# Attention, routed experts and a bilinear layer on one core: the last tokens' ranks, two weight loads, the w3 conversions and a padding moved

## The chip, the core and the metric

The kernel runs on one core of a Trainium2 chip. Its engines are TensorE (PE in the profile; PEld is its loading of weights), VectorE (DVE), ScalarE (ACT), GpSimd (POOL) and SyncE (SP), which here issues nearly all DMAs from one queue, in order. The metric is the device time of one execution in microseconds; less is better.

## The reference

Three layers follow each other, on 4 sequences of 576 tokens (N = 2304) with 512 features:

```python
# attention: 8 heads of 64, causal window of 128, linear bias per head, softmax
attn_out = _attn_ref(q, k, v)
x = attn_out.transpose(0, 2, 1, 3).reshape(B * S, H * D)

# experts: each token goes to one of 8
logits = x @ w_gate + modality_bias[modality_id]
e_idx = np.argmax(logits, axis=1)
gate_w = softmax(logits)[np.arange(N), e_idx]
for e in range(E):
    mask = e_idx == e
    h = np.maximum(x[mask] @ w1[e], 0.0)          # 512 -> 1024
    out[mask] = gate_w[mask, None] * (h @ w2[e])  # 1024 -> 512

# bilinear layer
a = x @ w1; b = x @ w2                            # 512 -> 1024
out = ((a * b) @ w3) @ w_out                      # 1024 -> 1024 -> 512
```

The weights of the bilinear layer come as float64 and are converted on the chip.

## The kernel before

All matrix products whose precision matters are done as three products of high and low parts: `split(hi, lo, src)` lets ACT write the high part (L264) and DVE the difference (L266), and `mm3` gives PE the three products (L281 to L283). A scheduler that simulates the engines orders the instructions of each engine from the order in the code and from `tc.issue_after(i)`, within which nothing is issued before the instruction i.

The stages of the program:

1. **Attention** (to about 222 us). For each unit (sequence, chunk of 128 tokens, four heads): scores, softmax, transposes, products with v. When a chunk is complete, `gate_logits(i, ...)` multiplies its output by the identity and the gate weights in one product (xlg); DVE multiplies by the reciprocal sums r and writes the token rows x and the gate's parts lh (L492); x goes to DRAM (xz, L502). Tiles 8 and 17 hold the 64-token tails of two sequences; there r is `one_r`, all ones, as the sums have been applied already. `route(g, ...)` takes a group of tiles: experts (hot_b, L531), counts before each tile (hcum, L536), ranks within the expert (rk, two products on PE, L540 and L543), positions (pos_i, L556), and scatters each token's number to its position in the list inv (POOL, L558). Group 4, the last, holds tiles 16 and 17.
2. **w3 times w_out** is prepared beside the attention, in pieces. `load_w3` brings piece i of w3 (float64, raw_w3_i; the profile writes raw_w) from DRAM by SP; `cvt_w3` converts it with five DVE instructions (w L694 and L698, p L701, x L704 and L707); `w3_transposes` has PE transpose it (w3tp_i, L739) and splits it (w3h_i, w3l_i); `w_step` adds its product to pw_j, which takes pieces 2j and 2j+1, and ACT copies pw out (wraw, L759). The list W_STEPS gives how many of these steps stand behind each attention unit; the rest follows behind the attention.
3. **The gap** (222 to 257 us). `block_table` computes from the counts which expert each block of 480 tokens takes (eb_i; eb0_i for the first), where its rows begin in the list (row_i, row0_i) and its columns (cols_i). SP reads these values from memory into registers (TENSOR_LOAD) before loads that depend on them: `load_w(g)` loads piece g of the expert weights (fw_g, 512 KB, L955), `gather_x(b)` loads block b's part of the list (ids_b, L975) and POOL gathers the token rows (xb, L981). `first_loads` issues the first list and then three pieces. `split_w` makes fwh and fwl of a piece, `block_transposes` transposes the gathered rows (btp, L1004) and splits them to xbh and xbl.
4. **Five blocks of experts** (257 to 450 us): ph and py are their products; the hidden part is kept in Whl. Beside them m's weights are converted.
5. **The bilinear layer** (to the end): products pS, pP, pA, pV, pG (L1296) with the weight pieces wth and wtl, and the output part po. Its weight pieces share their buffers with the expert pieces fwh and fwl (`f_p`).

SBUF is laid out by pools in stacks. `PAD` bytes per partition are reserved ahead of the pools of stages 3 to 5 on the left stack, so PAD moves all of their buffers.

Of the kernel before, what the change touches and what calls it, by code (L numbers as in the profile page):

```python
# [9 lines left out]
F32R = mybir.dt.float32r  # L10
# [4 lines left out]
ALU = mybir.AluOpType  # L15
# [3 lines left out]
P = 128  # L19
# [4 lines left out]
RU_LAST = 100  # L24
PAD = 32
NB_STATIC = 5
# [4 lines left out]
TP_AFTER = 20  # L31
LEAD = [4, 3, 1]
TS = 384
HB = 8
# [12 lines left out]
def kernel(  # L47
# [428 lines left out]
    def gate_logits(i, g, pos):  # L476
# [6 lines left out]
        for u in range(2):  # L483
            tp = pst("A", [P, 2, GW], f"xlg_{i}_{u}")
            for t in range(2):
                nc.tensor.matmul(
                    tp[:, t, :], lhsT=oT[:, 2 * u + t, :], rhs=wgx[:, 2 * u + t, :],
                    start=True, stop=True,
                )
            rr = r[:, 4 * u : 4 * u + 4].rearrange("p (t j o) -> p t j o", t=2, o=1)  # L490
            for dst, lo, n in ((lh, P, E), (x, 0, D)):
                nc.vector.tensor_tensor(  # L492
                    out=dst[:, 4 * u : 4 * u + 4, :].rearrange("p (t j) d -> p t j d", t=2),
                    in0=tp[:, :, lo : lo + 2 * n].rearrange("p t (j d) -> p t j d", j=2),
                    in1=rr.to_broadcast([P, 2, 2, n]), op=ALU.mult,
                )
# [7 lines left out]
    def route(g, i0, m):  # L504
# [30 lines left out]
        for j in range(i0, i0 + m):  # L535
# [6 lines left out]
        )  # L542
        nc.tensor.matmul(  # L543
            rk[:, :m, :], lhsT=ones_b, rhs=hcum[:, sl, :], start=False, stop=True
# [10 lines left out]
        )  # L555
        nc.vector.tensor_tensor(out=pos1_i[:, sl], in0=mn, in1=rank[:, sl], op=ALU.add)  # L556
        for j in range(i0, i0 + m):
# [175 lines left out]
    def w3_transposes(i):  # L733
        x = st_w.pop(("x", i))
        h = w_p.tile([P, 4, P], F32R, tag="w3h", name=f"w3h_{i}", bufs=3)
        l = w_p.tile([P, 4, P], F32R, tag="w3l", name=f"w3l_{i}", bufs=3)
        tp = pst("A", [P, 4, P], f"w3tp_{i}")
        for j in range(4):
            nc.tensor.transpose(tp[:, j, :], x[:, j * P : (j + 1) * P], ident)  # L739
        split(h, l, tp)  # L740
        st_w["last"] = (last["a"], last["v"])
        st_w["T", i] = (h, l)
# [127 lines left out]
    for i in range(nu + 2):  # L870
# [29 lines left out]
        for f in w_jobs.pop(i, []):  # L900
            f()
    todo += [lambda: None] * 4
    for i, f in enumerate(todo):
        f()
        for f in w_jobs.pop(nu + 2 + i, []):
            f()
    assert not w_jobs
    if j_in < n_j:
# [197 lines left out]

    def first_loads(b0, b1):

        gather_x(b0)
        with tc.issue_after(last["ids"].ins):  # L1110
            for g in range(b0 * NS, min(b0 * NS + LA, b1 * NS)):
                load_w(g)

    def run_blocks(b0, b1, extra, after=()):
# [8 lines left out]
        for b in range(b0, b1):  # L1123
            for s in range(NS):
                g = NS * b + s
                if g + LA < g1:
                    load_w(g + LA)
                if s == 0 and b + 1 < b1:
                    gather_x(b + 1)
                if s == 2:  # L1130
                    copy_ids(b)
# [19 lines left out]
    x_p = xstk.enter_context(tc.tile_pool(name="xp", bufs=2))  # L1151
    first_loads(0, NB_STATIC)
    for n in range(k_in, n_w):
        j, first = w_piece(n)
        if first:
            w3_transposes(j)
            if j + 2 < n_j:
                load_w3(j + 2)
            if j + 1 < n_j:
                cvt_w3(j + 1)  # L1160
        w_step(n)
# [104 lines left out]
    def split_wt(g, f, k):  # L1266
        h, l = (
            f_p.tile([P, 7, P], F32R, tag=f"w{x}", name=f"wt{x}_{g}_{f}_{k}", bufs=4) for x in "hl"
        )
        split(h, l, wt.pop(("raw", g, f, k)))  # L1270
        wt.setdefault((g, f), []).append((h, l))
# [287 lines left out]
```

## Time and profile before

| | |
|---|---|
| median of 3 runs | 762.26 us (760.52, 762.26, 768.61) |
| the profiled execution | 757.12 us |
| its span, first to last instruction | 755.4 us |
| mean granted clock of TensorE | 0.996 |
| PE busy | 734.9 us, 97% of the span |
| DVE busy | 526.2 us, 70% |
| ACT busy | 347.3 us, 46% |
| POOL busy | 74.9 us, 10% |
| DMA | 116.29 MB, 154 GB/s on average |

An engine's busy time is that of its instructions without the waits between them. The busy time of a pipelined instruction overlaps that of the next, so a distance from start to start can be shorter than the time of one. The granted clock is given as a share of 2.4 GHz.

### The profile page before, as it was taken

How to read it: one execution, taken by the hardware profiler on the slowest of the kernel's cores; microseconds unless marked ns; L12 is line 12 of the kernel's file. 1: busy time of each engine (PE TensorE's matmuls, PEld its weight loads, DVE VectorE, ACT ScalarE, POOL GpSimd, SP SyncE). 2: the span in 40 equal slices, each digit the busy share in tenths (PEclk: the TensorE clock that was granted, in tenths of full speed). 3: DMA queues.
4: the chain of work that ended last, by engine and by line, in shares of the span. 5: the costliest groups of instructions: out<-in, count | busy, mean ns of one | idle time of the engine just before them, and what ended most of it. 6: DMA issues, size and time to landing. Idle time of an engine off the chain costs nothing. (4 is left out here: it accounts for less than half of the span.)

```text
span 755.4 us, 12359 instructions
## 1 busy us (share of the span) xinstructions
PE 734.9 (97%) x4335; PEld 631.5 (84%) x4335; DVE 526.2 (70%) x1351; ACT 347.3 (46%) x778; POOL 74.9 (10%) x105
## 2 busy tenths in 40 slices
PE   7899999999999999999999999999999999999996
PEld 5777777787877788888888899999789997899984
DVE  3688888767689469697994347888657775568721
ACT  4787775866842533333343438231632315323221
POOL 5000200201013202030020000000120001100011
PEclk9999999999999999999999999999999999999999
DMA  7999467264136947979698344643226432233011
GB/s 132 325 312 252 109 179 178 67 161 129 44 84 149 253 144 222 293 196 352 180 297 268 132 133 116 209 123 98 77 71 192 123 96 77 67 118 116 1 43 42
DMA packets 126416, 116.29 MB, mean 154 GB/s; under 512 B 69631, under 2 KB 100735, under 8 KB 126344
## 3 DMA queue, kind: packets, MB, share of 16 engines
q1 hardware_dynamic: 122664, 105.91, 48.7%
q0 software_dynamic: 3680, 9.49, 4.0%
q8 instruction: 36, 0.59, 0.4%
q14 instruction: 36, 0.29, 0.1%
HBM read 87.69 MB, written 27.51 MB: 153 GB/s over the span
## 5 line engine op out<-in xcount | busy, mean ns | idle before, releaser
L264 ACT ACTIVATE wth<-wt 128x896 fp32r<-128x896 f32 x48 | 43.0, 946 | 89.6 <-PE pP L1296 89.6
L266 DVE TENSOR_TENSOR fwl<-fw,fwh 128x1024 fp32r<-128x1024 f32 x40 | 48.8, 1225 | 46.3 <-ACT fwh L264 45.8
L397 ACT ACTIVATE p<-p,mn 128x256 f32<-128x256 f32 (+2 forms) x144 | 68.1, 475 | 21.3 <-DVE mn L392 21.0
L264 ACT ACTIVATE fwh<-fw 128x1024 fp32r<-128x1024 f32 x40 | 42.1, 1062 | 76.6 <-PE ph L282 58.9
L281 PE MATMUL ph<-xbh,fwh 128*128 128x480 f32 (+1 forms) x160 | 60.1, 376 | 0.7 <-ACT xbh L264 0.7
L282 PE MATMUL py<-Whl,fwh 128*128 128x480 f32 (+1 forms) x160 | 59.9, 375 | 0.0
L282 PE MATMUL ph<-xbl,fwh 128*128 128x480 f32 (+1 forms) x160 | 59.7, 373 | 0.0
L283 PE MATMUL ph<-xbh,fwl 128*128 128x480 f32 (+1 forms) x160 | 59.6, 373 | 0.0
L283 PE MATMUL py<-Whl,fwl 128*128 128x480 f32 (+1 forms) x160 | 57.8, 373 | 0.0
L281 PE MATMUL po<-Whl,abh 128*128 128x512 f32 x144 | 57.1, 397 | 0.6 <-ACT abh L264 0.6
L283 PE MATMUL po<-Whl,abl 128*128 128x512 f32 x144 | 57.1, 398 | 0.0
L281 PE MATMUL py<-Whl,fwh 128*128 128x480 f32 (+1 forms) x160 | 56.9, 373 | 0.0
L282 PE MATMUL po<-Whl,abh 128*128 128x512 f32 x144 | 56.8, 394 | 0.0
L266 DVE TENSOR_TENSOR abl<-ab,abh 128x512 fp32r<-128x512 f32 x36 | 24.7, 690 | 40.7 <-ACT abh L264 40.6
L266 DVE TENSOR_TENSOR wtl<-wt,wth 128x896 fp32r<-128x896 f32 x48 | 51.8, 1083 | 1.6 <-ACT wth L264 1.4
L392 DVE CUSTOM_DVE_ANT_0 p<-S,bias 128x256 f32<-128x256 f32 (+1 forms) x128 | 43.8, 385 | 12.6 <-PE S L366 12.2
L1305 DVE TENSOR_TENSOR c<-pA,u 128x384 f32<-128x384 f32 x48 | 26.7, 557 | 33.9 <-PE pA L1296 31.7
L264 ACT ACTIVATE abh<-ab 128x512 fp32r<-128x512 f32 x36 | 22.5, 630 | 57.6 <-PE po L282 40.2
L454 PE MATMUL av<-pT,vr 128*64 128x128 f32 (+2 forms) x576 | 47.9, 275 | 0.0
L1401 POOL DMA_INDIRECT out_dram<-o,sid x18 | 21.6, 1200 | 262.9 <-ACT o L1400 262.9
L454 PEld LDWEIGHTS av<-pT,vr 128*64 128x64 f32 (+1 forms) x576 | 32.5, 136 | 11.5 <-issue 5.0
L418 PE MATMUL PT<-ident,p 128*128 128x128 f32 x224 | 41.0, 290 | 0.3
(256 smaller groups left out, 1944.6 us busy)
## 6 DMA issues: line engine op xcount, KB each, us to landing
wt<-wT SPq DMA_DIRECT2D x48, 448.0 KB, 3.3
fw<-in_moe_w_dram SPq DMA_DIRECT2D x40, 512.0 KB, 4.2
raw_w<-in_moe_w_dram SPq DMA_DIRECT2D x16, 512.0 KB, 5.1
raw_m<-in_moe_w_dram SPq DMA_DIRECT2D x32, 256.0 KB, 5.4
wT<-ms SPq DMA_DIRECT2D x16, 448.0 KB, 5.4
yT<-zf SPq DMA_DIRECT2D x20, 256.0 KB, 5.8
x<-yT SPq DMA_DIRECT2D x12, 384.0 KB, 5.5
vr<-in_v_dram SPq DMA_DIRECT2D x16, 256.0 KB, 4.6
```

Of the source, the lines that this page charges most:

```text
L264: last["a"] = nc.scalar.activation(out=hi, in_=src, func=AF.Copy, scale=scale)
L266: last["v"] = nc.vector.tensor_tensor(out=lo, in0=src, in1=f32(hi), op=ALU.subtract)
L281: nc.tensor.matmul(dst, lhsT=lh, rhs=rh, start=start, stop=False)
L282: nc.tensor.matmul(dst, lhsT=lh, rhs=rl, start=False, stop=False)
L283: return nc.tensor.matmul(dst, lhsT=ll, rhs=rh, start=False, stop=stop)
L392: nc.vector.tensor_tensor_reduce(out=p[:, j, t, :nk], in0=s[j][:, t, :nk], in1=bi, scale=1.0, scalar=BIG, op0=ALU.add, op1=ALU.min, accum_ ...
L397: nc.scalar.activation(out=p[:, j, t, :nk], in_=p[:, j, t, :nk], func=AF.Exp, scale=-1.0, bias=m1, accum_out=sm[:, col : col + 1],)
L418: nc.tensor.transpose(pt[:, t, kb, :], p[:, j, t, kb * P : (kb + 1) * P], ident)
L454: nc.tensor.matmul(av[j * D : (j + 1) * D, hp, cs], lhsT=raw["v", b, cc][:n_k, 2 * hp + j, :], rhs=rhs, start=(i_k == 0), stop=(i_k == len ...
L1305: last["d"] = nc.vector.tensor_tensor(out=out, in0=in0, in1=in1, op=op)
L1401: sc = nc.gpsimd.indirect_dma_start(out=out, out_offset=bass.IndirectOffsetOnAxis(ap=sid[g][:, j, 0:1], axis=0), in_=o, in_offset=None, bo ...
```

## The change

- In `gate_logits` x of the two tiles with r = one_r is copied by ACT, in two parts each, and no longer multiplied on DVE.
- `route` of the last group is taken out of the row of attention jobs and called ahead of the jobs of number `W_RANK` = 43, within an `issue_after` on the last transpose of the piece before; all later w3 jobs stand behind the last rank product (`last["rk"]`).
- The conversions of w3's pieces from j_in + 1 on are issued behind the last positions (`last["pos"]`).
- `first_loads` issues two weight pieces (SA = 2) and then the first list, in place of the list and three pieces (LA = 3). In `run_blocks` the next block's list is issued ahead of further weight pieces.
- PAD goes from 32 to 416 bytes. The tiles of the bilinear layer's weight pieces take the full slot of 1024 elements, and the pieces stand in it from element `WT_PAD` = 32 on. By the addresses, the offsets of fw, fwh and fwl within 512 bytes go from 416 to 288, those of xb, xbh and xbl from 480 to 352, those of the ab buffers from 96 to 480; wth and wtl stay at 416.

```diff
@@ -22,7 +22,8 @@
 NU, RU = 4, 120
 BLK = NU * RU
 RU_LAST = 100
-PAD = 32
+PAD = 416
+WT_PAD = 32
 NB_STATIC = 5
 NB_MAX = 12
 PE_LO = 9
@@ -30,6 +31,7 @@
 WO_AT = [9, 9, 12, 12, 12, 12, 14, 15]
 TP_AFTER = 20
 LEAD = [4, 3, 1]
+W_RANK = 43
 TS = 384
 HB = 8
 JS, BT = (2, 1)
@@ -488,7 +490,11 @@
                     start=True, stop=True,
                 )
             rr = r[:, 4 * u : 4 * u + 4].rearrange("p (t j o) -> p t j o", t=2, o=1)
-            for dst, lo, n in ((lh, P, E), (x, 0, D)):
+            if r is one_r:
+                nc.scalar.copy(
+                    x[:, 4 * u : 4 * u + 4, :].rearrange("p (t j) d -> p t (j d)", t=2), tp[:, :, :P]
+                )
+            for dst, lo, n in ((lh, P, E), (x, 0, D))[: 1 if r is one_r else 2]:
                 nc.vector.tensor_tensor(
                     out=dst[:, 4 * u : 4 * u + 4, :].rearrange("p (t j) d -> p t j d", t=2),
                     in0=tp[:, :, lo : lo + 2 * n].rearrange("p t (j d) -> p t j d", j=2),
@@ -540,7 +546,7 @@
         nc.tensor.matmul(
             rk[:, :m, :], lhsT=tri_b, rhs=hot_b[:, sl, :], start=True, stop=False
         )
-        nc.tensor.matmul(
+        last["rk"] = nc.tensor.matmul(
             rk[:, :m, :], lhsT=ones_b, rhs=hcum[:, sl, :], start=False, stop=True
         )
         nc.vector.tensor_reduce(out=sm, in_=ex, axis=AX.X, op=ALU.add)
@@ -553,7 +559,9 @@
         nc.vector.tensor_scalar(
             out=mn, in0=mn, scalar1=float(E), scalar2=float(CAP), op0=ALU.add, op1=ALU.mult
         )
-        nc.vector.tensor_tensor(out=pos1_i[:, sl], in0=mn, in1=rank[:, sl], op=ALU.add)
+        last["pos"] = nc.vector.tensor_tensor(
+            out=pos1_i[:, sl], in0=mn, in1=rank[:, sl], op=ALU.add
+        )
         for j in range(i0, i0 + m):
             sc = nc.gpsimd.indirect_dma_start(
                 out=inv2, out_offset=bass.IndirectOffsetOnAxis(ap=pos1_i[:, j : j + 1], axis=0),
@@ -736,7 +744,7 @@
         l = w_p.tile([P, 4, P], F32R, tag="w3l", name=f"w3l_{i}", bufs=3)
         tp = pst("A", [P, 4, P], f"w3tp_{i}")
         for j in range(4):
-            nc.tensor.transpose(tp[:, j, :], x[:, j * P : (j + 1) * P], ident)
+            st_w["t"] = nc.tensor.transpose(tp[:, j, :], x[:, j * P : (j + 1) * P], ident)
         split(h, l, tp)
         st_w["last"] = (last["a"], last["v"])
         st_w["T", i] = (h, l)
@@ -899,12 +907,19 @@
             todo.pop(0)()
         for f in w_jobs.pop(i, []):
             f()
-    todo += [lambda: None] * 4
-    for i, f in enumerate(todo):
+
+    *todo, route_last = todo
+    for f in todo:
         f()
-        for f in w_jobs.pop(nu + 2 + i, []):
+    for i in sorted(w_jobs):
+        if i == W_RANK:
+            with tc.issue_after(st_w["t"].ins):
+                route_last()
+            behind_rank = ExitStack()
+            behind_rank.enter_context(tc.issue_after(last["rk"].ins))
+        for f in w_jobs.pop(i):
             f()
-    assert not w_jobs
+    behind_rank.close()
     if j_in < n_j:
         load_w3(j_in)
         cvt_w3(j_in)
@@ -1104,12 +1119,11 @@
 
     LA, SA = 3, 2
 
-    def first_loads(b0, b1):
-
-        gather_x(b0)
-        with tc.issue_after(last["ids"].ins):
-            for g in range(b0 * NS, min(b0 * NS + LA, b1 * NS)):
-                load_w(g)
+    def first_loads():
+
+        for g in range(SA):
+            load_w(g)
+        gather_x(0)
 
     def run_blocks(b0, b1, extra, after=()):
         g0, g1 = b0 * NS, b1 * NS
@@ -1123,10 +1137,11 @@
         for b in range(b0, b1):
             for s in range(NS):
                 g = NS * b + s
-                if g + LA < g1:
-                    load_w(g + LA)
                 if s == 0 and b + 1 < b1:
                     gather_x(b + 1)
+                for n in range(SA if g == g0 else LA, LA + 1):
+                    if g + n < g1:
+                        load_w(g + n)
                 if s == 2:
                     copy_ids(b)
                 if g + SA < g1:
@@ -1149,7 +1164,7 @@
 
     xstk = ExitStack()
     x_p = xstk.enter_context(tc.tile_pool(name="xp", bufs=2))
-    first_loads(0, NB_STATIC)
+    first_loads()
     for n in range(k_in, n_w):
         j, first = w_piece(n)
         if first:
@@ -1157,7 +1172,8 @@
             if j + 2 < n_j:
                 load_w3(j + 2)
             if j + 1 < n_j:
-                cvt_w3(j + 1)
+                with tc.issue_after(last["pos"].ins) if j > j_in else nullcontext():
+                    cvt_w3(j + 1)
         w_step(n)
     w3_last = st_w["last"]
     wstk.close()
@@ -1265,7 +1281,10 @@
 
     def split_wt(g, f, k):
         h, l = (
-            f_p.tile([P, 7, P], F32R, tag=f"w{x}", name=f"wt{x}_{g}_{f}_{k}", bufs=4) for x in "hl"
+            f_p.tile([P, 2 * DM], F32R, tag=f"w{x}", name=f"wt{x}_{g}_{f}_{k}", bufs=4)[
+                :, WT_PAD : WT_PAD + 7 * P
+            ].rearrange("p (s c) -> p s c", s=7)
+            for x in "hl"
         )
         split(h, l, wt.pop(("raw", g, f, k)))
         wt.setdefault((g, f), []).append((h, l))
```

The first place is **PE** between the two halves of product pw_4. Here rk_4 are the ranks, w3tp_9 the transposes of piece 9, w3h_9 and w3l_9 its parts, tri_b and ones_b constants. Before:

```order
L283 MATMUL pw_4_3300<-woh_110,w3l_8_3258 128x512
L540 LDWEIGHTS tri_b_74
L540 MATMUL rk_4_3323<-hot_b_86,tri_b_74 128x16
L739 MATMUL w3tp_9_3344<-ident_70,x_w3_9_3268 128x128 x4
L543 LDWEIGHTS ones_b_73
L543 MATMUL rk_4_3323<-hcum_85,ones_b_73 128x16
L281 MATMUL pw_4_3300<-woh_110,w3h_9_3342 128x512
L282 MATMUL pw_4_3300<-wol_111,w3h_9_3342 128x512
```

After:

```order
L285 MATMUL pw_4_3300<-woh_110,w3l_8_3258 128x512
L747 MATMUL w3tp_9_3315<-ident_70,x_w3_9_3268 128x128 x4
L546 LDWEIGHTS tri_b_74
L546 MATMUL rk_4_3338<-hot_b_86,tri_b_74 128x16
L549 LDWEIGHTS ones_b_73
L549 MATMUL rk_4_3338<-hcum_85,ones_b_73 128x16
L283 MATMUL pw_4_3300<-woh_110,w3h_9_3313 128x512
L284 MATMUL pw_4_3300<-wol_111,w3h_9_3313 128x512
```

The transposes stood between the two rank products; they now stand ahead of both.

The second place is **DVE** from the rank products to the first values of the block table. Of w3's pieces, w_w3, p_w3 and x_w3 are the steps of a conversion; pr and rank lead to the positions pos1_i, f0 and cm belong to the block table. Before:

```order
L704 SCALAR_TENSOR_TENSOR x_w3_12_3530<-raw_w3_12_3494,p_w3_12_3529 128x512
L550 TENSOR_TENSOR pr_4_3310<-rk_4_3323,onehot_84 128x16
L266 TENSOR_TENSOR w3l_9_3343<-w3tp_9_3344,w3h_9_3342 128x512
L707 TENSOR_TENSOR x_w3_12_3530<-x_w3_12_3530,w_w3_12_3528 128x512
L701 TENSOR_SCALAR p_w3_13_3561<-w_w3_13_3560 128x512
L551 TENSOR_REDUCE rank_83<-pr_4_3310 128x2
L577 SCALAR_TENSOR_TENSOR fe_3378<-cnt_3376,iota_em_81 128x8
L586 COPY cnt_s_3384<-cnt_3376 128x8
L694 TENSOR_SCALAR w_w3_14_3592<-raw_w3_14_3558 128x512
L556 TENSOR_TENSOR pos1_i_82<-mnx_4_3313,rank_83 128x2
L580 TENSOR_REDUCE f0_3379<-fe_3378 128x1
L589 TENSOR_TENSOR cm_3389<-cnt_s_3384,thr_113 128x40
```

After:

```order
L556 TENSOR_TENSOR pr_4_3325<-rk_4_3338,onehot_84 128x16
L268 TENSOR_TENSOR w3l_9_3314<-w3tp_9_3315,w3h_9_3313 128x512
L557 TENSOR_REDUCE rank_83<-pr_4_3325 128x2
L585 SCALAR_TENSOR_TENSOR fe_3378<-cnt_3376,iota_em_81 128x8
L594 COPY cnt_s_3384<-cnt_3376 128x8
L562 TENSOR_TENSOR pos1_i_82<-mnx_4_3328,rank_83 128x2
L702 TENSOR_SCALAR w_w3_12_3526<-raw_w3_12_3492 128x512
L588 TENSOR_REDUCE f0_3379<-fe_3378 128x1
L597 TENSOR_TENSOR cm_3389<-cnt_s_3384,thr_113 128x40
L702 TENSOR_SCALAR w_w3_13_3558<-raw_w3_13_3524 128x512
L706 SCALAR_TENSOR_TENSOR w_w3_12_3526<-raw_w3_12_3492,w_w3_12_3526 128x512
L589 TENSOR_SCALAR eb0_i_89<-f0_3379 128x1
```

The conversions of pieces 12 to 14 that stood ahead of the positions now stand behind them, between the instructions of the block table. Further ahead, between the lh of tile 17 and hot_b, two of piece 13 and the two copies of x are gone.

The third place is **SP's queue** from the stores of the last token rows on. TENSOR_LOAD reads a register. Before:

```order
L502 DMA xz_98<-x_17_3283 64x512 x2
L680 DMA raw_w3_15_3590<-in_moe2_w3_dram 128x1024
L972 TENSOR_LOAD row0_i_90
L972 ISA x2
L975 ISA
L975 DMA ids_0_3460<-inv2_99 120x4x2
L944 TENSOR_LOAD eb0_i_89
L944 ISA x2
L955 ISA
L955 DMA fw_0_3479<-in_moe_w1_dram 128x4x256
L955 ISA
L955 DMA fw_1_3481<-in_moe_w1_dram 128x4x256
```

After:

```order
L508 DMA xz_98<-x_17_3283 64x512 x2
L959 TENSOR_LOAD eb0_i_89
L959 ISA x2
L970 ISA
L970 DMA fw_0_3460<-in_moe_w1_dram 128x4x256
L970 ISA
L970 DMA fw_1_3462<-in_moe_w1_dram 128x4x256
L987 TENSOR_LOAD row0_i_90
L987 ISA x2
L990 ISA
L990 DMA ids_0_3473<-inv2_99 120x4x2
L688 DMA raw_w3_15_3588<-in_moe2_w3_dram 128x1024
```

The load of raw_w3_15 has moved from right behind the stores to behind the first list, and the first two weight pieces stand ahead of the list. Further on, ids_1 stands ahead of fw_2 and fw_3 and not behind them. On ACT the order of the last pieces is nearly the same as before: w3h_15, fwh_0 to fwh_3, xbh_0, then the copy of pw_7. In the attention stage, from the first tile with one_r on, the scheduler gives another order of the same products on PE.

## Rows read from the trace of the kernel before

**Rows 1.** Windows: length, busy us and count of each engine, granted clock, DMA.
```profile
0.00:220.00 220.00, 212.11 (x1698) 165.55 (x1698) 166.40 (x687) 154.49 (x488) 22.78 (x58) 1.00 0.63 166
...
230.00:234.00 4.00, 4.00 (x16) 3.13 (x15) 3.49 (x24) 0.59 (x2) 2.41 (x3) 0.60 0.51 118
...
257.20:755.40 498.20, 489.20 (x2466) 439.80 (x2466) 329.45 (x563) 179.87 (x268) 38.95 (x34) 1.00 0.48 148
```

**Rows 2.** Timeline of PE at the first ph: start, length, idle before.
```profile
257.10 0.70 PE L281 MATMUL ph<-xbh,fwh 128*128 128x480 f32 x2 [0.66 <-ACT xbh L264]
```

**Rows 3.** Timeline of PE at the ranks.
```profile
225.60 0.39 PE L283 MATMUL pw<-woh,w3l 128*128 128x512 f32 x1
227.09 0.18 PE L540 MATMUL rk<-hot_b,tri_b 128*128 128x16 bf16 x1 [1.10 <-DVE hot_b L531]
227.13 0.63 PE L739 MATMUL w3tp<-ident,x_w 128*128 128x128 f32 x4
...
228.45 0.50 PE L281 MATMUL pw<-woh,w3h 128*128 128x512 f32 x1 [0.68 <-ACT w3h L264]
```

**Rows 4.** Timeline of DVE at the ranks.
```profile
223.63 0.42 DVE L492 TENSOR_TENSOR x<-xlg,one_r 128x256 f32<-128x256 f32 x1
...
224.72 0.69 DVE L698 SCALAR_TENSOR_TENSOR w_w<-raw_w,w_w 128x512 int32<-128x512 int32 x1
225.32 0.27 DVE L498 TENSOR_REDUCE lsum<-lh 128x8 f32<-128x64 f32 x1
...
230.58 0.15 DVE L556 TENSOR_TENSOR pos_i<-mnx,rank 128x2 int32<-128x2 f32 x1
```

**Rows 5.** Timeline of DVE in the second half of the gap.
```profile
242.27 0.16 DVE L630 TENSOR_TENSOR row_i<-r,eb 128x12 int32<-128x12 f32 x1
...
249.66 4.63 DVE L266 TENSOR_TENSOR fwl<-fw,fwh 128x1024 fp32r<-128x1024 f32 x4 [0.25 <-ACT fwh L264]
254.21 0.65 DVE L266 TENSOR_TENSOR xbl<-btp,xbh 128x480 fp32r<-128x480 f32 x1
```

**Rows 6.** Timeline of ACT at the first weight pieces.
```profile
248.57 3.90 ACT L264 ACTIVATE fwh<-fw 128x1024 fp32r<-128x1024 f32 x4
```

**Rows 7.** Timeline of SP's queue: start and length of issues.
```profile
236.63 0.43 SPq L975 DMA_DIRECT2D ids<-inv  x1
...
243.35 0.39 SPq L975 DMA_DIRECT2D ids<-inv  x1
```

**Rows 8.** Timeline of POOL: the last scatter of group 4.
```profile
232.65 0.96 POOL L558 DMA_INDIRECT inv<-tg,pos_i  x1 [0.30 <-DMA xz<-x]
```

**Rows 9.** Issues from 220, 228, 232.5, 236, 238, 243 us on: KB, us to landing.
```profile
xz<-x SPq DMA_DIRECT2D x2, 128.0 KB, 7.4
...
raw_w<-in_moe_w_dram SPq DMA_DIRECT2D x1, 512.0 KB, 5.9
...
inv<-tg,pos_i POOLq DMA_INDIRECT x1, 3.7
...
ids<-inv SPq DMA_DIRECT2D x1, 3.8 KB, 1.8
...
fw<-in_moe_w_dram SPq DMA_DIRECT2D x1, 512.0 KB, 3.6
...
xb<-xz,ids POOLq DMA_INDIRECT x2, 8.4
ids<-inv SPq DMA_DIRECT2D x1, 3.8 KB, 8.3
```

**Rows 10.** Timeline of PE in products pw_5 and pw_7: two starts of each.
```profile
235.68 0.39 PE L281 MATMUL pw<-woh,w3h 128*128 128x512 f32 x1
...
236.61 0.39 PE L282 MATMUL pw<-wol,w3h 128*128 128x512 f32 x1
...
249.04 0.40 PE L281 MATMUL pw<-woh,w3h 128*128 128x512 f32 x1
...
249.95 0.39 PE L282 MATMUL pw<-wol,w3h 128*128 128x512 f32 x1
```

## The prediction

> **What bounds the kernel now.** I read the windows first: TensorE (PE) is the bound. From 257.2 us to the end it is busy 489.20 of 498.20 us, and it idles 7.9 of the first 220 us [rows 1]. A change that keeps the amount of PE's work can pay where PE waits or runs at a low clock, and all edits but the padding aim at one such place, between the last attention products and the first product of the expert blocks, ph, at 257.10 [rows 2]. Next I read PE's timeline there. After the product at 225.60 it waits 1.10 us for hot_b (the one-hot experts of the last tokens), does a rank product and four transposes of w3's piece 9, and then waits 0.68 us for w3h_9, so the next product starts only at 228.45 [rows 3]. In 230 to 234 us, shortly after these two waits, its granted clock is 0.60 of full speed on average [rows 1], which is the 1.2 GHz level for four fifths of that time, 3.2 us, and the 2.4 GHz level for the rest. Work of 3.2 us at the low level takes 1.6 at the high one, so 1.6 us are lost. At the end of the gap ph waits 0.66 us for xbh, with shorter waits ahead of it. The holes and the slow stretch together are worth some 7 us, 0.9% of the time, and this is all that the order around the gap can give.
>
> **The ranks between transposes and products.** PE finishes the product of 225.60 at about 225.83. Now the transposes of piece 9 follow at once, and their product comes 1.32 us after the first transpose (228.45 - 227.13 [rows 3]): 227.15, a gain of 1.30 us. hot_b must then be there by 226.3, when the transposes end. Before, its matmul started at 227.09; the two x copies, 0.42 us of VectorE (DVE) each, have gone to ScalarE (ACT), so it is there by 226.25 even if nothing else moved, and of the w3 conversions at least the wide one of 0.69 us [rows 4] went too. No wait is left there. ACT does nothing else at that moment, and its two copies lie ahead of w3h_9, so they cost nothing.
>
> **The conversions behind the positions.** A wide conversion is 0.60 us from start to start (224.72 to 225.32), a narrow one 0.42 less the same 0.08 of overlap, 0.34 [rows 4]. Moved from ahead of pos_i to behind it are piece 12 whole (2 narrow, 3 wide: 2.48), three instructions of piece 13 (1.28) and one of piece 14 (0.34): 4.1 us. Ahead of pos_i DVE has w3l_9, which follows w3h_9, 1.3 earlier; between that and pos_i 1.2 us of conversions have gone. pos_i: 230.58 - 1.3 - 1.2 = 228.1. But the 4.1 us come back right behind it. From pos_i to row_i, the last input of the SP queue's next loads, it was 242.27 - 230.58 = 11.7 us [rows 4, 5]; it is 15.8 now, so row_i comes at 243.9, **1.6 later** than before. This is what the edit gives back.
>
> **Two weight pieces ahead of the list.** Four things on SP's queue now stand in another order. (a) fw_0 and fw_1 go out as soon as their expert is known and x_17 is stored, whose stores took 7.4 us to land [rows 9]: about 232, where fw_0 went behind 238 [rows 9]. (b) The list ids_0 needs the second scatter of inv, which was issued 2.07 us behind pos_i (232.65) and landed 3.7 later [rows 7 to 9]: 230.2 and 233.9. With the two issues and a register load ahead of it ids_0 goes out at 234.2 to 235.3 instead of 236.63 [rows 7]. (c) raw_w3_15 stood ahead of all these, issued between 228 and 229 [rows 9], and now stands **behind** ids_0: 234.6 to 235.7. (d) fw_2 and fw_3 stand behind row_i and ids_1. ids_1 was issued 1.08 us behind row_i (243.35); so fw_3 goes out at 243.9 + 1.1 + 1.0 = 246.0.
>
> Both (c) and (d) have someone waiting. For (c) it is DVE: piece 15's conversion stands, by my count, 9.9 us behind pos_i (pieces 12 and 13 whole, 5.0; three instructions of 14, 1.3; w3l_10 to w3l_12, 1.8; some twenty small ones, 1.9), so it is due at 238.0. The load's landing has two bounds: 3.6 us as fw_0's, the same 512 KB into a quiet machine, and 5.9 as raw_w3_15's own among the stores [rows 9]. That is 238.2 to 241.6. I take 3.6 and some contention from fw_1's tail, 239.3, since the other transfers will have ended: a stall of 1.3 us (0.2 to 3.6). Behind the stalled instruction on DVE stand the rest of row_i's chain, w3l_13 and the last two pieces' x; row_i and with it (d) move by the same amount. PE has products until about 242 and so feels it only through these.
>
> For (d) it is ACT, whose queue is in order: fwh_2 and fwh_3 stand ahead of xbh_0. fw_3 lands 3.6 to 4.4 behind its issue, 250.2 taken, and with the stall 251.5. Then fwh_3 takes 0.98 us (3.90 for four [rows 6]), fwl_3 1.16 (4.63 for four), and from the first xbl to ph it was 257.10 - 254.21 = 2.89 [rows 2, 5]. **First ph: 251.5 + 5.05 = 256.55, 0.55 earlier than before** (255.45 to 258.85 with the stall's bounds). The 1.3 us and the slow stretch that PE gets back early in the gap are thus lost again in waiting for ph; they don't add to the 0.55.
>
> On (a) a rule speaks against the edit. First the row: ids_1, 3.8 KB, took 8.3 us beside four weight loads, ids_0 with nothing beside it 1.8 [rows 9]. The Trainium skill ("Trainium Kernel Development and Optimization", Key Constraints) says that DMAs of all queues run on the same 16 engines and interleave, so that a list behind two weight pieces would pay as ids_1 did; the trace agrees with it in these two rows. What that would do here is the third rival.
>
> **The padding.** Buffers of the blocks shift by 384 bytes, while the bilinear stage's weight pieces keep their offset. If an address mattered to PE it would show in the pace. Products of one kind, from the same pool of buffers, are 0.2275 us apart at 249.04 to 249.95 (4 steps) and 0.2325 at 235.68 to 236.61 (4 steps) [rows 10]. So the rows show 2% of spread where the addresses are alike, and none that an address explains. I take 0, with bounds of 1% of the 489 us in either direction, 5 us.
>
> **The attention stage.** From the first tile of mixed sequences on, the scheduler gives other orders on PE, with the same instructions. DVE loses four copies (1.7 us), ACT gains four, and neither is the bound. With 7.9 us of idle there in all, I take 0, and 2 us either way as a quarter of that idle.
>
> **The rivals.** (1) **The late w3 piece decides: slower.** The place is DVE's wait for raw_w3_15, the price 1 us of ph per us of landing; it turns to a loss from 239.85 on, the stall of 1.85 that brings ph back to 257.10. For it: 6 us later on the queue, and an early need. Landing at 241.6 gives +1.75, and if it takes the 8.3 us of ids_1, at 243.5, +3.6 us: 764 to 766. (2) **No stall**, and fw_3 lands at 248 since the machine is quiet: ph at 253 to 254.5, limited by PE and fwh, so 3 to 4 us: 758.8. Against it: row_i's 1.6. (3) **The list pays for the weights**: ids_0 at 235 + 8.3 = 243.3 instead of 238.40; the last gathers, issued between 243 and 244 and 8.4 us in landing [rows 9], so some 13 us behind the list, come at 256.4, and ph at 258: +1, 763.3. (4) **The padding changes PE's pace** by 1% or more: 755 to 757 or 766 to 768. It is the only one with leverage on 489 us. (5) **The change does not do what it says**: the clock falls all the same in the new order, since waits for w3h_10 and w3h_15 stay. As ph is set by the weights this costs nothing more: as the forecast.
>
> **How the numbers follow.** The sum is -0.55 (gap) + 0 + 0. The profiled execution took 757.12 us (span 755.4 and 1.7 around it) and would take 756.6; it stands 5.1 us under the median of the three runs, so I put the difference on the median: 762.26 - 0.55 = **761.7**. Chances: forecast with (5) 0.40, (1) 0.20, (2) 0.13, (3) 0.10, (4) 0.17, of which 0.10 on the fast side and 0.07 on the slow. The runs spread over 8 us (760.52 to 768.61), so some 1% (7.6 us) is what a measurement can tell from no change. The range reaches from (4) fast to (4) slow with the attention stage's 2 us in part: 755.5 to 767. Over 1% faster needs the padding, or (2) with a good attention stage: 0.13. Over 1% slower needs the padding or (1) at its worst with a bad one: 0.10. Within: 0.77.
>
> **What would show it.** Right: the rank products directly behind piece 9's transposes, without idle time ahead; the first product of w3h_9 at about 227.2; pos_i near 228.1; fw_0 issued near 232; DVE idle 1 us for raw_w near 238; ACT waiting for fw between fwh_1 and fwh_2; ph at 256 to 257; equal pace of ph, py and po. Wrong: ph before 254.5 (then weights or list landed earlier than I have it) or after 259 (raw_w or ids), or products after ph closer or farther apart than before, which would be the padding's doing. A first 220 us that differ by over 3 us would mean that the order in the attention stage was worth more than I gave it.

## The result, and the profile after

The changed kernel takes 769.19 us (median of 22 runs, 763.5 to 776.5) against 763.33 (22 runs, 758.7 to 768.61). The ratio, in which disturbed runs are left out on both sides, is 1.0063, with an interval of 1.0037 to 1.0089: 4.8 us slower (2.8 to 6.8). The forecast was 0.55 us faster, within a range that ended at 767; the median lies 2.2 us above it.

The profiled execution has a span of 765.9 us, 10.5 over that of before. Three marks cut it: the first product of tile 8's gate (xlg, at 129.26 before and 133.03 after), the last product of tile 17's gate, and the first ph. PE's timeline of the kernel before has the second mark, and two products of the last stage that are ten apart:

```profile
223.04 0.65 PE L486 MATMUL xlg<-wgx,oTt 128*128 128x144 f32 x4
...
739.61 0.39 PE L282 MATMUL po<-Whl,abh 128*128 128x512 f32 x1
...
741.94 0.40 PE L283 MATMUL po<-Whl,abl 128*128 128x512 f32 x1
```

PE's timeline of the changed kernel, at the ranks (as [rows 3]), at ph (as [rows 2]), and two po products that are eight apart:

```profile
230.04 0.65 PE L488 MATMUL xlg<-wgx,oTt 128*128 128x144 f32 x4
...
232.62 0.39 PE L285 MATMUL pw<-woh,w3l 128*128 128x512 f32 x1
232.85 0.60 PE L747 MATMUL w3tp<-ident,x_w 128*128 128x128 f32 x4
233.28 0.17 PE L546 MATMUL rk<-hot_b,tri_b 128*128 128x16 bf16 x1
233.33 0.17 PE L549 MATMUL rk<-hcum,ones_b 128*128 128x16 bf16 x1
234.13 0.50 PE L283 MATMUL pw<-woh,w3h 128*128 128x512 f32 x1 [0.64 <-ACT w3h L266]
...
265.39 1.86 PE L1019 MATMUL btp<-ident,xb 120*128 120x120 f32 x8 [3.34 <-DVE xbl L268]
267.92 1.17 PE L283 MATMUL ph<-xbh,fwh 128*128 128x480 f32 x2 [0.66 <-ACT xbh L266]
...
749.00 0.39 PE L284 MATMUL po<-Whl,abh 128*128 128x512 f32 x1
...
750.81 0.39 PE L283 MATMUL po<-Whl,abh 128*128 128x512 f32 x1
```

- To tile 8: +3.8. The order on every engine is that of before up to there. In this execution the clock fell near 30 us (0.83 on average from 20 to 40 us, 1.00 before); in the padding alone it fell at 119 us and tile 8 is at 132.59, in the run without copies it did not fall and tile 8 is at 129.37. I put this down to the execution and not to the change, since the order is the same and since the timed runs (2.8 to 6.8) have no room for the whole 10.5; it is not shown. Of the profiles, all six with the copies have a fall of the clock ahead of tile 8, and three of the eight others.
- Tile 8 to the last xlg: 93.8 before, 97.0 after, **+3.2**, with the clock at 1.00 in both. The order of PE's products is what differs here (`copies_alone`, below).
- The last xlg to ph, the gap: 34.06 before, 37.88 after, **+3.8**. The wait for hot_b at the ranks is gone as planned (0.64 us for w3h are left), and a new hole of 3.34 us stands ahead of ph.
- ph to the end: 498.3 before, 498.0 after. Two things nearly cancel here: po is 0.233 us apart before (10 steps) and 0.226 after (8 steps), and the clock fell behind the hole. The windows (columns as in [rows 1]) of the changed kernel:

```profile
232.00:237.00 5.00, 4.37 (x23) 3.34 (x22) 4.40 (x28) 0.81 (x2) 1.17 (x2) 1.00 0.43 105
...
262.00:267.90 5.90, 1.92 (x9) 1.49 (x8) 3.02 (x5) 3.61 (x6) 1.97 (x2) 0.71 0.92 273
267.90:272.00 4.10, 4.08 (x12) 3.38 (x13) 0.66 (x1) 0.00 (x0) 0.98 (x1) 0.58 1.05 344
272.00:276.00 4.00, 4.00 (x20) 3.48 (x19) 0.80 (x2) 1.81 (x3) 0.00 (x0) 1.00 0.61 152
```

At the ranks, behind which the clock was 0.60 before [rows 1], it is 1.00 now; it falls at the hole ahead of ph instead, and the first ph products run at 1.2 GHz: 12 products in the 4.1 us from 267.9 on, and 20 in the next 4.0.

Where the new hole comes from is on SP, DVE and ACT. SP's queue (as [rows 7]), DVE (as [rows 4, 5]) and ACT (as [rows 6]) of the changed kernel, each in a fence:

```profile
238.13 1.03 SPq L970 DMA_DIRECT2D fw<-in_moe_w_dram  x2
241.56 0.41 SPq L990 DMA_DIRECT2D ids<-inv  x1
242.02 0.42 SPq L688 DMA_DIRECT2D raw_w<-in_moe_w_dram  x1
255.00 0.39 SPq L990 DMA_DIRECT2D ids<-inv  x1
255.59 3.51 SPq L970 DMA_DIRECT2D fw<-in_moe_w_dram  x3
```

```profile
235.10 0.15 DVE L562 TENSOR_TENSOR pos_i<-mnx,rank 128x2 int32<-128x2 f32 x1
...
247.98 0.43 DVE L702 TENSOR_SCALAR w_w<-raw_w 128x512 int32<-128x512 int32 x1 [3.10 <-DMA raw_w<-in_moe_w_dram]
...
254.08 0.17 DVE L638 TENSOR_TENSOR row_i<-r,eb 128x12 int32<-128x12 f32 x1
```

```profile
259.57 1.06 ACT L266 ACTIVATE fwh<-fw 128x1024 fp32r<-128x1024 f32 x1 [2.90 <-DMA fw<-in_moe_w_dram]
262.46 1.06 ACT L266 ACTIVATE fwh<-fw 128x1024 fp32r<-128x1024 f32 x1 [1.83 <-DMA fw<-in_moe_w_dram]
```

raw_w3_15, issued at 242.02, lands so late that DVE waits 3.10 us; row_i is late; fw_2 and fw_3 go out behind row_i; and ACT, which has them ahead of the token rows, waits 2.90 and 1.83 us. In the issues from 238, 241.4, 242 and 255.5 us on (as [rows 9]) the transfers took:

```profile
fw<-in_moe_w_dram SPq DMA_DIRECT2D x2, 512.0 KB, 7.2
...
ids<-inv SPq DMA_DIRECT2D x1, 3.8 KB, 5.1
...
raw_w<-in_moe_w_dram SPq DMA_DIRECT2D x1, 512.0 KB, 5.9
...
fw<-in_moe_w_dram SPq DMA_DIRECT2D x3, 512.0 KB, 4.6
```

Behind the issue of fw_0 (238.13 in the changed kernel, 238.12 before) hardly anything moved for 4.4 us: 27 GB/s, the last number of a window's line, where the kernel before moved 240 in the same stretch. The changed kernel:

```profile
238.10:242.50 4.40, 3.96 (x18) 2.77 (x17) 4.40 (x16) 0.95 (x2) 0.00 (x0) 1.00 0.40 27
242.50:247.50 5.00, 4.76 (x26) 3.78 (x24) 2.38 (x7) 1.69 (x3) 0.00 (x0) 1.00 0.89 292
```

The kernel before:

```profile
238.10:242.50 4.40, 4.40 (x27) 3.68 (x26) 4.40 (x17) 1.94 (x4) 2.61 (x3) 1.00 0.71 240
```

### The profile page after: what moved, and what is told of

Its sections match the earlier page's. It is cut to its first block, busy times and chain, and to the rows that moved or that the text cites. A ratio compares the mean times of both kernels' runs of the same rounds, so it can differ in the third digit from the quotient of the medians.

```text
span 765.9 us, 12364 instructions
## 1 busy us (share of the span) xinstructions
PE 739.6 (97%) x4335; PEld 634.6 (83%) x4335; DVE 524.7 (69%) x1347; ACT 349.4 (46%) x782; POOL 73.8 (10%) x105
## 5 line engine op out<-in xcount | busy, mean ns | idle before, releaser
L456 PE MATMUL av<-pT,vr 128*64 128x128 f32 (+2 forms) x576 | 50.8, 279 | 0.0
L266 ACT ACTIVATE abh<-ab 128x512 fp32r<-128x512 f32 x36 | 22.5, 629 | 56.4 <-PE po L284 39.0
L456 PEld LDWEIGHTS av<-pT,vr 128*64 128x64 f32 (+1 forms) x576 | 34.2, 138 | 12.7 <-issue 6.1
```

Of the source, the lines that this page charges most:

```text
L266: last["a"] = nc.scalar.activation(out=hi, in_=src, func=AF.Copy, scale=scale)
L456: nc.tensor.matmul(av[j * D : (j + 1) * D, hp, cs], lhsT=raw["v", b, cc][:n_k, 2 * hp + j, :], rhs=rhs, start=(i_k == 0), stop=(i_k == len ...
```

## The experiments

Theory A, from the two traces: the loss is the attention order (some 3 us) and the gap (some 4 us and a fall of the clock), and the padding gains 2. Rivals: the padding does nothing or costs; the attention order is neutral; one edit alone makes the gap's loss. The ratios are to before, each kernel with 12 runs (`no_loads` with 6). "Gap" is the time from the last xlg to the first ph in the profiled execution, 34.06 in before and 37.88 in the changed kernel.

**The padding alone** (`pad_alone`), on the kernel before:

```diff
-PAD = 32
+PAD = 416
+WT_PAD = 32
```

with the bilinear pieces at element 32 of a full slot, as in the change.

> The kernel before with the padding alone (416 bytes, the bilinear weight pieces kept at their offset). Every engine's order is that of before. Theory A (the loss of the changed kernel lies in the attention order and in the gap, and the padding makes PE's products run closer together, as its trace shows for po): po at about 227 ns apart in place of 232, py at 215 to 216 in place of 218, ph as before, so 2 to 4 us faster than before, ratio 0.995 to 0.997. Theory B (the padding does nothing, and the pace differs from run to run): ratio 0.999 to 1.001 and po at 232. Theory C (the padding is what costs): ratio over 1.002.

Ratio 0.9967 (0.9936 to 0.9997), 759.98 us. From ph to the end it takes 496.3 us against 498.3, and no clock fall is in either ahead of the last 6 us. po stands 0.226 apart (740.04 to 741.85, 8 steps). Theory A holds here; that the padding does nothing falls. The five other profiles that have the padding and no fall behind ph agree, 496.1 to 496.6. The gap of this kernel is 35.27, 1.2 us longer than before in the same order, though its clock stays at 1.00. So gaps of two single profiles that differ by about 1 us show nothing, and a full clock behind the ranks alone brought ph no earlier.

**The copies alone** (`copies_alone`), on the kernel before: the hunk of `gate_logits`.

> The kernel before with the four copies of x on ACT alone. On PE it has the attention order of the changed kernel but for 6 rows. Theory A (that order costs some 3 us between 115 and 230 us): 2 to 4 us slower than before, ratio 1.003 to 1.005, with the last xlg product some 3 us later and the gap as long as before or a little shorter, as hot_b comes earlier. Theory D (the order is neutral, and the profiled run of the changed kernel was late at the ranks only because of a fall of the clock near 30 us): the last xlg within 1 us of before when both have the same clock falls, ratio 0.998 to 1.001.

Ratio 1.0078 (1.0042 to 1.0115), more than expected. From tile 8 to the last xlg it takes 99.3 us against 93.8; of these 5.5, about 2.6 are a fall of the clock in this execution (0.97 granted there, 1.00 before). The gap is 36.14: it is not shorter, although hot_b has less ahead of it. The neutral order falls. Where it costs is read in the two kernels whose clock is 1.00 in the stage, before and changed. PE from tile 8 to the last xlg, before:

```profile
129.26:223.04 93.78, 93.65 (x823) 74.95 (x820) 70.18 (x317) 65.30 (x213) 10.67 (x11) 1.00 0.38 97
```

The changed kernel, and the three holes of PE in it:

```profile
133.03:230.04 97.01, 95.63 (x823) 75.42 (x819) 68.15 (x313) 66.33 (x216) 10.77 (x12) 1.00 0.40 94
...
141.93 0.18 PE L546 MATMUL rk<-hot_b,tri_b 128*128 128x40 bf16 x1 [0.39 <-DVE hot_b L537]
...
214.95 0.33 PE L420 MATMUL PT<-ident,p 128*128 128x128 f32 x1 [0.41 <-ACT pT L421]
...
223.99 0.30 PE L425 MATMUL PT<-ident,p 128*128 128x128 f32 x1 [0.58 <-DVE p L408]
```

PE is idle for 1.38 us in place of 0.13, and busy for 1.98 us longer. Most of the latter is in the products with v. The page has them for the whole kernel, before and after the change (busy us, mean ns, idle before):

```profile
L454 PE MATMUL av<-pT,vr 128*64 128x128 f32 (+2 forms) x576 | 47.9, 275 | 0.0
```

```profile
L456 PE MATMUL av<-pT,vr 128*64 128x128 f32 (+2 forms) x576 | 50.8, 279 | 0.0
```

Between the two marks alone they are busy for 23.00 and 24.85 us. So the new order costs 1.2 us by new holes, and some 2 us since the same products, in another mix, take longer; why they do is open. `copies_alone` has the same three holes.

**The change without the copies** (`no_copies`): that hunk undone.

> The changed kernel with x of the mixed tiles on DVE again, all else changed. On PE it has the attention order of before but for 14 rows near its end. Theory A: faster than the changed kernel by the 3 us of that order, so ratio to before 1.001 to 1.004, the last xlg near 223 to 224 us when the clock does not fall early, and a gap that is as bad as in the changed kernel (ph about 38 us behind the last xlg, DVE waiting 2 to 4 us for raw_w). Theory D: ratio as the changed kernel's, 1.005 to 1.008, as all its loss is in the gap.

Ratio 1.0054 (1.0021 to 1.0087). Tile 8 to the last xlg is back at 93.3 us, the gap at 37.85 as in the changed kernel, with a clock of 0.75 and 0.50 around ph. So the gap's loss does not need the copies. The time fell less than I expected, and the intervals of 1.0054 and 1.0063 overlap.

**The change without the loads' edit** (`no_loads`): `first_loads` and `run_blocks` as before.

> The changed kernel with the list and then three weight pieces ahead, as before, all else changed. Theory A for the gap (raw_w3_15 behind the list, and fw_2 and fw_3 behind row_i, make DVE and ACT wait): without either wait ph stands 34 us behind the last xlg or less, against 37.9, so 3 to 7 us faster than the changed kernel (the upper end if the fall of the clock behind ph goes too): ratio to before 0.998 to 1.003. Rival E (the conversions behind the positions hold the gap back whatever the loads do, since row_i comes later and raw_w3_12's buffer is free later): ph still 37 us or more behind the last xlg, ratio 1.005 or more.

Ratio 1.0125 (1.0073 to 1.0177), the slowest of all, gap 38.81. Rival E: the conversions hold the gap back. DVE and PE of this kernel:

```profile
253.87 0.43 DVE L702 TENSOR_SCALAR w_w<-raw_w 128x512 int32<-128x512 int32 x1 [4.75 <-DMA raw_w<-in_moe_w_dram]
```

```profile
258.08 1.08 PE L747 MATMUL w3tp<-ident,x_w 128*128 128x128 f32 x4 [4.41 <-DVE wide L667]
```

Here raw_w3_15 stands behind ids_0 and three weight pieces (issued at 245.38), DVE waits 4.75 us for it, and PE waits 4.41 for the transposes. The reason is its buffer, as the next run shows. There are three for raw_w; piece 15 takes that of piece 12, and with piece 12's conversion behind the positions it comes free so late that the scheduler puts other loads ahead.

**Conversions from piece 13 on** (`cvt13`), on the changed kernel:

```diff
-                with tc.issue_after(last["pos"].ins) if j > j_in else nullcontext():
+                with tc.issue_after(last["pos"].ins) if j > j_in + 1 else nullcontext():
```

> The changed kernel, with the conversions behind the positions from piece 13 on in place of piece 12. Piece 12 is then converted ahead of the positions, raw_w3_15 has its buffer early and stands again right behind the stores on SP's queue, ahead of the weight pieces and the list; the attention order, the loads and the padding are those of the changed kernel. Theory F (the gap's loss is raw_w3_15's late issue, which comes from the buffer that piece 12 holds): DVE no longer waits for raw_w near its conversion, fw_2 and fw_3 are issued some 3 us earlier relative to the last xlg, ph 33 to 35 us behind the last xlg instead of 37.5, 3 to 5 us faster than the changed kernel: ratio to before 1.000 to 1.003 (the attention order's 3 us less the padding's 2 remain). Rival G (row_i comes late in any case, and with it fw_2 and fw_3): ph 36.5 us or more behind the last xlg, ratio 1.004 to 1.008.

Ratio 1.0101 (1.0065 to 1.0138), gap 36.59. raw_w3_15 goes out ahead of the weights, and DVE no longer waits for it, so that part of theory F is right; but rival G decides the time, which lies above G's 1.008 too. ACT and PE:

```profile
264.49 1.06 ACT L266 ACTIVATE fwh<-fw 128x1024 fp32r<-128x1024 f32 x1 [2.79 <-DMA fw<-in_moe_w_dram]
267.81 1.06 ACT L266 ACTIVATE fwh<-fw 128x1024 fp32r<-128x1024 f32 x1 [2.26 <-DMA fw<-in_moe_w_dram]
```

```profile
270.75 1.06 PE L1019 MATMUL btp<-ident,xb 120*128 120x120 f32 x4 [4.85 <-DVE xbl L268]
272.47 1.17 PE L283 MATMUL ph<-xbh,fwh 128*128 128x480 f32 x2 [0.66 <-ACT xbh L266]
```

fw_2 and fw_3 behind row_i and ids_1 are a second cause, which works without the first. The windows of this kernel show 0.74 and 0.59 of the clock around ph again.

**The change without the conversions' edit** (`no_cvt`): `cvt_w3(j + 1)` as before.

> The changed kernel without the edit of the conversions, all else changed. Theory F: as the run with the conversions from piece 13 on, ph 33 to 35 us behind the last xlg, ratio 1.000 to 1.003. Rival H (the two pieces ahead of the list cost by themselves, through the list's landing or through fw_2 and fw_3 behind row_i and ids_1): ph 36 us or more behind the last xlg with ACT waiting for fw, ratio 1.004 or more.

Ratio 1.0059 (1.0024 to 1.0094), gap 38.43: against theory F. The rank matmul now waits 3.27 us for hot_b, since more conversions stand ahead of it on DVE, and the clock falls at that hole; ACT waits 2.2 us for fw too.

**Ranks and padding** (`rank_pad`), on the kernel before: the hunks of `W_RANK` and of the padding.

> The kernel before with the padding and with the rank products behind the transposes, nothing else: the attention order and SP's queue are those of before. Expected if the waits at the ranks are worth what the prediction said (1.3 us, and 1.6 more if the clock stays up there): ratio 0.993 to 0.996, ph 31 to 33 us behind the last xlg. If the gap is held by the list, the weights or the gathers and not by the ranks: as the padding alone, 0.996 to 0.998.

Ratio 0.9993 (0.9963 to 1.0022), gap 36.53. The gain of the padding is no longer seen, though the two intervals overlap. PE at the ranks:

```profile
236.32 0.18 PE L542 MATMUL rk<-hot_b,tri_b 128*128 128x16 bf16 x1 [4.45 <-DVE hot_b L533]
```

Of [rows 3] the wait was 1.10. The scheduler, told that the ranks come late, put conversions ahead of hot_b. Neither expectation had this.

**The same with the loads** (`rank_loads_pad`): the hunks of `first_loads` and `run_blocks` as well.

> The same with the two weight pieces ahead of the list, and the list of the next block ahead of fw_2: attention order of before, conversions as before, raw_w3_15 right behind the stores. Theory F: like the run without the loads' edit, within 0.3%. Rival H: slower than that by 0.3 to 0.6%, with ACT waiting 2 us or more for fw and ph 2 to 4 us later behind the last xlg.

Ratio 1.0067 (1.0031 to 1.0104), gap 37.82, with ACT waiting 2.8 us for fw and PE 3.05 for xbl: rival H, 0.7% by the loads' edit alone. The gap is only 1.3 us longer than that of `rank_pad`, and not the 2 to 4 expected; here the clock falls behind ph.

**The gap repaired** (`cvt13_rank_pad`): the kernel before with the padding, the ranks and the conversions from piece 13 on; copies and loads as before.

> The kernel before with the padding, the rank products behind the transposes, and the conversions behind the positions from piece 13 on; x on DVE and the loads as before. raw_w3_15 stands right behind the stores, fw_0 to fw_3 right behind the first list. If the late raw_w3_15, the late fw_2 and fw_3 and the attention order are the whole loss of the changed kernel, this keeps what is good in it: no wait for raw_w, none for fw, ph 31.5 to 34 us behind the last xlg, 2 to 4 us faster than before: ratio 0.993 to 0.997. If the rank edit or the conversions cost by themselves (row_i later, the gathers later), ph is 35 us or more behind and the ratio 0.998 or more.

Ratio 0.9949 (0.9916 to 0.9983), 759.38 us: faster than both kernels. Gap 32.54. That the order adds to what the padding gives is not shown by the timed runs: the padding alone has 0.9967, and the intervals overlap. PE at the ranks and at ph, and two windows:

```profile
226.27 0.60 PE L743 MATMUL w3tp<-ident,x_w 128*128 128x128 f32 x4
227.74 0.18 PE L542 MATMUL rk<-hot_b,tri_b 128*128 128x16 bf16 x1 [0.87 <-DVE hot_b L533]
229.07 0.17 PE L545 MATMUL rk<-hcum,ones_b 128*128 128x16 bf16 x1 [1.15 <-DVE hcum L538]
...
256.02 0.70 PE L283 MATMUL ph<-xbh,fwh 128*128 128x480 f32 x2 [0.66 <-issue]
```

```profile
228.00:234.00 6.00, 4.75 (x24) 3.33 (x23) 5.82 (x24) 1.68 (x3) 2.38 (x3) 1.00 0.67 91
...
245.00:256.10 11.10, 9.64 (x52) 7.62 (x50) 7.37 (x10) 7.53 (x11) 2.95 (x3) 1.00 0.83 232
```

The ranks still wait 2 us here, but the clock stays up, and no hole of several us stands ahead of ph.

**The same without the ranks' edit** (`cvt13_pad`).

> The same without the rank edit: the rank products stand around the transposes as before. If that edit is worth its 1.3 us here, this is 0.1 to 0.4% slower than the run with it; if hot_b comes so late that the products behind the ranks wait either way, they are the same within 0.1%.

Ratio 0.9949 (0.9921 to 0.9978), gap 35.38 in its profile. The ranks' edit is worth nothing that can be measured here, but not for the reason expected, a wait for hot_b in both: at the ranks PE waits 0.18 us for hot_b and 0.68 for w3h in this kernel, and 0.87 for hot_b and 1.15 for hcum in the one with the edit.

**Two pieces ahead of the list, two behind it** (`cvt13_two_two`), on the repaired kernel:

```diff
+        for g in range(SA):
+            load_w(g)
         gather_x(0)
+        for g in range(SA, LA + 1):
+            load_w(g)
```

> As the first of this call, with two weight pieces ahead of the first list and fw_2 and fw_3 right behind it (so not behind row_i and ids_1, as in the changed kernel). If the loss of the loads' edit is fw_2 and fw_3 behind row_i: no ACT wait for fw of over 1 us, ph as in the first of this call within 1 us, the same ratio within 0.2%. If it is the two pieces ahead of the list: ids_0 and the gathers later, btp or xbh waits, ph 1 us or more later, ratio 0.2% or more above.

Ratio 0.9973 (0.9941 to 1.0004), gap 34.18. ACT has no wait for fw; so the great loss of the loads' edit is fw_2 and fw_3 behind row_i. If the two pieces ahead cost something, it is 0.2%, within the intervals. ph is 1.6 us later than in the repaired kernel, over the 1 us that I had set for that, but the profiles differ in the clock: PE has the same waits at the ranks in both (0.87 and 1.15), and behind them the clock fell here and not there.

```profile
230.00:234.00 4.00, 4.00 (x16) 2.92 (x14) 2.58 (x11) 0.89 (x2) 1.94 (x3) 0.57 0.43 58
```

At 0.57 these 4 us hold the work of 2.3. That is as much as the 1.6, so the two pieces need not be its cause.

**The repaired kernel with the copies** (`cvt13_copies_rank_pad`).

> As the first of this call, with the four copies of x on ACT, so with the attention order of the changed kernel and its gap repaired. If that order costs 3 to 4 us between the first mixed tile and the last xlg: ratio 0.4 to 0.6% above the first of this call, and the last xlg 97 us or more behind the first mixed tile's in place of 94. If the copies' relief of DVE pays at the ranks, up to 1 us less.

Ratio 0.9978 (0.9945 to 1.0010), gap 32.74, tile 8 to the last xlg 97.0 us. The order of the attention stage costs 3.2 us in the profile and 0.3% in the medians, where the intervals overlap, again with av at 50.7 and the three holes. This kernel differs from `cvt13` in the loads alone, 1.0101, and from `no_loads` in piece 12's conversion alone, 1.0125: either edit costs over 1% by itself in that company.

## Why the prediction was wrong

Shifted by the 7.0 us by which the last xlg is later, the steps ahead of the gap's end came as written. The rank products stand behind the transposes without a wait, and the next product came 1.28 us after the first of these (1.32). pos_i was due at 235.1 and came at 235.10, ids_0 at 241.2 to 242.3 and 241.56, raw_w3_15's issue at 241.6 to 242.7 and 242.02. That DVE would want it 9.9 us behind pos_i was right as well: 247.98 - 3.10 is 9.8 behind. row_i, with the stall that was measured, was due at 254.0 and came at 254.08.

What failed:

- **The landing of raw_w3_15.** I took 3.6 us and some contention, as fw_0's in the quiet machine [rows 9]. It took 5.9, the other bound: a stall of 3.10 in place of 1.3. This is rival (1), to which I gave 0.20: over its turning point of 1.85. The step that failed is that the transfers ahead would have ended. fw_0 and fw_1 went out at 238.13 and 238.78, but moved next to nothing until 242.5, so raw_w3_15, issued at 242.02, ran beside both: they took 7.2 us where fw_0 took 3.6, and ids_0 5.1 where it took 1.8. The rule that I had weighed there (the Trainium skill, "Trainium Kernel Development and Optimization", Key Constraints: DMAs of all queues share 16 engines and interleave) agrees with the rows from 242.5 on, where these loads share 292 GB/s; I had applied it to the list alone. Why fw_0 and fw_1 started so late, with 27 GB/s in motion, stays open. `no_copies` shows it again: 26 GB/s in the 4.4 us behind fw_0's issue, and DVE waiting 3.54 us for raw_w.
- **The landing of fw_3.** I took it 4.2 us behind an issue at 246.0, which is 256.1 and 260.3 with shift and stall. The issue came in time, at 256.18 in the group of three from 255.59 on, but ACT got it at 262.46, 6.3 us behind it. From there to ph I had 5.05 and it was 5.46. The longer stall (1.8), the later landing (2.2) and the way to ph (0.4) make the gap +3.8 in place of -0.55.
- **A term was missing: the fall of the clock at the new hole.** I had priced the slow stretch at the ranks as something that can go, and wrote that it costs nothing if it falls all the same. It fell at the hole and stayed low behind ph, where PE is the bound: about 1.7 us, the difference of 498.0 to the 496.3 of the padding alone. The six profiles with the padding and a fall behind ph have 498.0 to 498.7 there, the six without a fall 496.1 to 496.6.
- **The attention stage at 0.** It is +3.2. I looked for idle time that a new order could fill or open, and it did open 1.2 us; the larger part is that the same products took longer, for which I had no term. The bound of 2 us, a quarter of the idle time, was no bound on that.
- **The padding at 0.** It is -2.0 from ph to the end. I compared products of one kind in one pool, in [rows 10], and not po with pw, which have other offsets.

One sum of the prediction does not come out, though nothing hung on it: between the last xlg and ph PE is idle for 3.6 us (34.06 less 30.48 busy), which with the 1.6 of the slow stretch makes 5.2 and not some 7.

The terms as the profile has them, -2.0, +1.7, +3.2 and +3.8, come to 6.7; the timed runs say 4.8 (2.8 to 6.8). The range ended at 767 since its slow end was built from the padding and a part of the attention stage's 2 us; a loss in the gap and one in the attention stage together lay beyond it. Not settled, besides the late start of fw_0, is how the gap's loss divides in the changed kernel itself: either cause alone gives it in other company (`no_loads`, `cvt13`), and together they are no worse. And `cvt13` lies above the changed kernel, which I can't explain beyond the overlap of their intervals.

## What to carry to other kernels

A load's place in the queue is set by when its buffer comes free, so an instruction that is moved back on a compute engine can move a load, and behind it everything on an in-order queue: follow the buffers of a moved step, not only its own time. Ahead of the stage that PE bounds, a hole can be dearer than its length, since the clock may fall behind it; fill the last hole first. An edit that hands a scheduler a freedom is to be timed alone, as the ranks' edit gave 4.45 us of new wait without its companion, and four copies reordered a stage that had nothing to do with the aim.

## What the runs showed that I had not expected

- **Where operands lie changes PE's pace.** With 384 bytes of padding po goes from 0.233 to 0.226 us a product, and the median from start to start of py from 0.218 to 0.215; ph and the products with wth stay at 0.217 and 0.173. The median of po is 0.227 in all twelve profiles with the padding, and 0.231 and 0.232 in the two without. By the addresses, po's second operand (abh, abl) went from 96 to 480 within 512 bytes, with Whl at 480; ph's two operands moved together. That it is the difference of the two offsets fits these four and was not tried further.
- **The same products take longer in another mix**: from tile 8 to the last xlg av is busy for 22.5 to 23.1 us with the old order, in eight profiles, and for 24.8 to 25.3 with the new one, in six.
- **The time of an execution goes with the granted clock.** Of the changed kernel, 763.5 us went with a mean of 0.996, 767.6 with 0.989, 771.8 with 0.981. Between the last xlg and ph the fourteen profiles have eleven holes of PE of 2.15 to 4.85 us, and the clock fell in each of them or right behind it. Behind shorter ones it fell in one execution and not in another: at the ranks in the kernel before (1.10 and 0.68 us) and not in the padding alone (1.11 and 0.68), and ahead of ph in `cvt13_two_two`, with holes of 0.51, 0.29 and 0.66 us (0.66 of the clock in 257 to 262), and not in the kernel before, with 0.53, 0.27 and 0.66. So a long hole is not needed, and a short one is not enough.
